# Two FNet and GLU layers on one core: the tests that stand between the matrices, spread otherwise over the steps

## The chip, the cores and the metric

One core of one Trainium2 chip runs the kernel; the other cores are idle. The metric is the device time of one execution in microseconds. Three runs of the kernel before took 1140.98, 1141.98 and 1143.59 us, so the median is 1141.98 us. One more execution was profiled and took 1143.76 us.

## The reference

Two layers, each a spectral mixing and a gated linear unit, on x of 2048 rows by 640 columns, all in float32:

```python
def _A_ref(x, dft_seq_re, dft_seq_im, dft_hid_re, dft_hid_im):
    a = jnp.einsum("bsd,ed->bse", x, dft_hid_re)
    b = jnp.einsum("bsd,ed->bse", x, dft_hid_im)
    return jnp.einsum("ts,bse->bte", dft_seq_re, a) - jnp.einsum("ts,bse->bte", dft_seq_im, b)

def _B_ref(x, w_gate, w_up, w_down):
    h = _sigmoid(jnp.einsum("bsd,df->bsf", x, w_gate)) * jnp.einsum("bsd,df->bsf", x, w_up)
    return jnp.einsum("bsf,fd->bsd", h, w_down)

for _ in range(2):
    x = x + _A_ref(_layernorm(x), ...)
    x = x + _B_ref(_layernorm(x), ...)
```

The two sequence matrices have 2048 by 2048 numbers, the two hidden matrices 640 by 640, and the three weights of the unit have 1728 hidden columns. All of them are inputs. The kernel uses that the four transform matrices are symmetric in their rows and columns, and it does not take that for granted: while it computes by the short way it tests these symmetries on the data, sums up the squares of all deviations, and at the end goes to a general way (`general`) if a flag says that one of them does not hold.

## The kernel before, in words

**The matrices.** Numbers are split into a high and a low half-precision part (HI and LO), and a product is made of three passes. The 2048 rows are four blocks (`block` holds the step at which each begins). A block has 14 steps in which gate and up values are made, two hidden chunks j to a pair of steps, and then eight steps that multiply by the third weight (`down`, matrices at L1546, drained by VectorE at L1561). Layer 1's blocks 1, 2 and 3 begin at steps 19, 41 and 63, layer 2's four blocks at steps 105, 127, 149 and 171.

**A pair of steps in TensorE's order.** For two chunks come parts one (6 matrices each) and two (9 each), then the gates of the pair before, then part four of one older chunk (9), part six twice (6 each), part four of the other (9), part five twice (6 each), part seven twice (9 each) and part three twice (9 each): 108 matrices of 128 by 256, nearly all at L1389. After parts five, six and seven ScalarE copies the sums out of PSUM (L1393, a snap). Part seven needs part six's snap, and part three needs part five's. After part three VectorE adds (L1425, L1426), which also frees the banks; ScalarE makes the gate from that (L1435). The up values go through VectorE (L1445, L1447) and are split by ScalarE (L1456) and VectorE (L1457).

**The order is written out.** The function that holds all this first lists the steps and then places small jobs with `at(u, f, ...)`: job f runs at place u, a number of steps with a fraction. When a step is emitted, its jobs are sorted by u. A down step emits them ahead of its matrices. A pair of steps has four places for them, numbered 0 to 3 by the halves of its two steps: place 0 stands behind the gates and ahead of part six, place 1 after part six, place 2 after part five, place 3 after part seven and ahead of part three. Each engine works through its own instructions in the order in which they were emitted, so a job that waits holds up what stands behind it on its engine.

**The tests.** A test has three jobs. `load_rows` or `load_cols` fetches four pieces of a sequence matrix (`in_ct`) with four DMAs that GpSimd issues (L1596, L1613). `test_rows` or `test_cols` takes differences and sums on VectorE (L1602, L1603 and L1605 twice; for columns L1619 to L1622). `square_rest` takes the oldest entry of the list `rest` and squares it on ScalarE with a running sum (L1579). The data lie in a room of 8 units of SBUF; there are two rooms, and test k uses room k modulo 2. So a load waits for the square of the test two before it. In layer 1 there are 42 tests from step 47 to step 76 and 9 more in the last phase of the layer; the load is at u, the test one pace later and the square 1.7 paces after the load, a pace being the distance between two tests. In layer 2 the rest come in three runs: 8 in block 0, 10 in block 1, 15 around block 2, the test 1.4 and the square 1.8 paces after the load.

**The hidden matrices.** `load_hidden_rows` (GpSimd) and `load_hidden_cols` (SyncE) fetch them into the same two rooms in block 2's second half and block 3; `test_hidden_rows` and `test_hidden_cols` (L1679, L1682, L1683) test them on VectorE. `test_all` makes the flag from all sums (L1693 to L1710).

**Buffers.** Everything else in SBUF that lives for a while is taken from `Slots`: a first pass over the program writes down how long each slot is held on a clock that advances with every take and give, and `find_homes` then places all slots, the largest area first.

## Time and profile before

| what | value |
|---|---|
| median of three runs | 1141.98 us |
| the profiled execution | 1143.76 us, its span 1141.9 us |
| TensorE busy | 1110.8 us, 97% |
| VectorE busy | 761.8 us, 67% |
| ScalarE busy | 537.2 us, 47% |
| GpSimd busy | 348.1 us, 30% |
| granted TensorE clock, mean | 0.996 |
| DMA | 214.72 MB, 188 GB/s in the mean |

A row of a timeline gives the start and the length of one instruction or of a run of like ones in us, the engine, the line of the kernel, the operation and its operands, and in brackets how long the engine was idle ahead of it and what ended that. A row of the costliest groups gives the busy time, the mean of one in ns, and the idle time ahead of them. A row of windows gives, after the window and its length, the busy time of TensorE, of its weight loads, of VectorE, ScalarE and GpSimd with the number of instructions, the clock, the share of the DMA engines and GB/s. Line numbers are those of the kernel before; in the changed kernel the same code stands one line further down, and beyond the test functions up to 13.

### The profile page before, as it was taken

The page shows a single profiled execution, that of the slowest core. Times are in us where ns is not written, and L with a number is a line of the kernel's source. Part 1 is how long each engine was busy: PE and PEld are TensorE (multiplying, and loading weights), DVE is VectorE, ACT ScalarE, POOL GpSimd, SP SyncE. Part 2 cuts the span into 40 slices and gives each one's busy share as a digit, 9 for nine tenths or more (in the row PEclk, how much of TensorE's full clock was granted, in tenths as well). Part 3 has the DMA queues.
Part 4 walks back from the last instruction along what each step waited for, and adds up shares of the span by engine and source line. Part 5 has one row for each costly group of instructions (what it writes and reads, how often), then busy time and mean ns, then how long its engine had stood idle before and what let it go on. Part 6 is the DMA issues. An engine that isn't in the chain of part 4 may idle for free. (4 is left out here: it accounts for less than half of the span.)

```text
span 1141.9 us, 23440 instructions
## 1 busy us (share of the span) xinstructions
PE 1110.8 (97%) x9030; PEld 882.3 (77%) x9030; DVE 761.8 (67%) x1678; ACT 537.2 (47%) x1187; POOL 348.1 (30%) x568
## 2 busy tenths in 40 slices
PE   5889999999999999999999999999999999999998
PEld 3668446788878887788878888778877888788875
DVE  7994998856756775486667878834664568526750
ACT  6975583355524653256525545315541455225430
POOL 1001664332546452432350216021453113141000
PEclk9899999999999999999999999999999999999999
DMA  8444685967495767968621665475767864499401
GB/s 250 152 124 151 240 319 157 270 210 244 154 244 182 246 185 152 246 223 291 201 98 57 177 223 160 130 216 179 241 167 174 257 230 150 85 254 284 143 18 38
DMA packets 154447, 214.72 MB, mean 188 GB/s; under 512 B 74655, under 2 KB 99505, under 8 KB 154326
## 3 DMA queue, kind: packets, MB, share of 16 engines
q1 hardware_dynamic: 135622, 165.04, 48.4%
q0 software_dynamic: 18560, 47.93, 14.3%
q8 instruction: 72, 1.18, 0.4%
q14 instruction: 49, 0.40, 0.1%
q10 hardware_dynamic: 144, 0.16, 0.0%
HBM read 173.04 MB, written 25.44 MB: 174 GB/s over the span
## 5 line engine op out<-in xcount | busy, mean ns | idle before, releaser
L1389 PE MATMUL acc<-big 128*128 128x256 f16 x4698 | 517.1, 273 | 4.7 <-ACT big L1393 4.5
L1389 PEld LDWEIGHTS <-big 128*128 128x128 f16 x4698 | 459.6, 98 | 60.1 <-issue 5.7
L1546 PE MATMUL acc<-big 128*128 128x320 f16 x2624 | 357.7, 299 | 0.0
L1546 PEld LDWEIGHTS <-big 128*128 128x128 f16 x2624 | 256.8, 98 | 99.5
L1596 POOL DMA_DIRECT2D big<-in_ct x256 | 174.5, 687 | 270.6 <-DVE big L1605 181.3
L1393 ACT ACTIVATE big<-acc 128x256 f32<-128x256 f32 x348 | 127.7, 380 | 214.7 <-PE acc L1389 212.4
L1579 ACT ACTIVATE big<-big 128x768 f32<-128x768 f32 (+10 forms) x110 | 81.6, 742 | 113.0 <-DVE big L1605 85.5
L1457 DVE TENSOR_TENSOR big<-big 128x512 f16<-128x512 f32 x87 | 59.9, 689 | 105.9 <-ACT big L1456 105.7
L1342 PE MATMUL acc<-big 128*128 128x256 f16 (+1 forms) x705 | 114.6, 325 | 0.5 <-ACT big L672 0.5
L1342 PEld LDWEIGHTS <-big 128*128 128x128 f16 x705 | 68.9, 98 | 45.0 <-issue 0.7
L1435 ACT ACTIVATE big<-big 128x512 f32<-128x512 f32 x87 | 53.3, 627 | 49.1 <-DVE big L1426 48.2
L270 DVE SCALAR_TENSOR_TENSOR big<-big 128x640 f16<-128x640 f32 (+7 forms) x82 | 62.7, 797 | 6.7 <-ACT big L268 6.6
L1561 DVE SCALAR_TENSOR_TENSOR big<-acc,big 128x320 f32<-128x320 f32 x64 | 28.4, 483 | 57.8 <-PE acc L1546 57.8
L1445 DVE SCALAR_TENSOR_TENSOR big<-acc,big 128x256 f32<-128x256 f32 x87 | 36.3, 418 | 41.7 <-PE acc L1389 36.3
L1426 DVE TENSOR_TENSOR big<-big,acc 128x512 f32<-128x512 f32 x87 | 59.2, 681 | 2.0 <-PE acc L1389 1.8
L268 ACT ACTIVATE big<-big 128x640 f16<-128x640 f32 (+7 forms) x82 | 50.9, 657 | 17.3 <-POOL big L1283 6.5
L616 ACT ACTIVATE big<-big 128x384 f16<-128x384 f32 (+2 forms) x48 | 28.8, 648 | 64.1 <-DVE big L598 45.0
L1456 ACT ACTIVATE big<-big 128x512 f16<-128x512 f32 x87 | 54.5, 626 | 9.3 <-DVE big L1447 7.3
L1613 POOL DMA_DIRECT2D big<-in_ct x40 | 27.3, 685 | 96.9 <-ACT big L1393 73.7
L1602 DVE TENSOR_TENSOR big<-big 128x256 f32<-128x256 f32 x64 | 26.7, 416 | 27.4 <-DMA big<-in_ct 26.0
L1603 DVE TENSOR_TENSOR big<-big 128x256 f32<-128x256 f32 x64 | 26.9, 420 | 21.9 <-DMA big<-in_ct 21.9
L979 PE MATMUL acc<-big 128*128 128x256 f16 (+2 forms) x288 | 34.7, 273 | 6.4 <-DVE big L270 2.5
(242 smaller groups left out, 1068.3 us busy)
## 6 DMA issues: line engine op xcount, KB each, us to landing
big<-kept_s SPq DMA_DIRECT2D x84, 512.0 KB, 5.7
big<-kept_w SPq DMA_DIRECT2D x115, 320.0 KB, 5.3
big<-in_ct POOLq DMA_DIRECT2D x256, 128.0 KB, 4.4
big<-kept_w SPq DMA_DIRECT2D x74, 192.0 KB, 6.2
kept_w<-big SPq DMA_DIRECT2D x27, 320.0 KB, 3.7
big<-in_ct POOLq DMA_DIRECT2D x32, 256.0 KB, 4.9
kept_s<-big SPq DMA_DIRECT2D x13, 512.0 KB, 5.7
big<-in_wg SPq DMA_DIRECT2D x18, 320.0 KB, 3.2
```

The costliest lines, as they stand in the source:

```text
L268: nc.scalar.activation(dh, src, AF.Copy, scale=s)
L270: nc.vector.scalar_tensor_tensor(dl, src, s, dh, op0=OP.mult, op1=OP.subtract)
L1342: nc.tensor.matmul(ps, w[wp][:, d * P : (d + 1) * P], xt[:, xp, :], start=(d == 0 and wp == HI and xp == HI), stop=(d == ND - 1 and wp == LO))
L1389: nc.tensor.matmul(ps, wt, xt, start=start and n == 0, stop=n == len(todo) - 1, skip_group_check=not start)
L1393: nc.scalar.activation(dst, ps, AF.Copy)
L1426: nc.vector.tensor_tensor(v, v, other, op=OP.add)
L1435: nc.scalar.activation(v, v, AF.Sigmoid, scale=SG)
L1456: nc.scalar.activation(s.parts[HI], v, AF.Copy)
L1457: nc.vector.tensor_tensor(s.parts[LO], v, s.parts[HI], op=OP.subtract)
L1546: nc.tensor.matmul(held["pd", e][0][:, :EH], held["ht", j].parts[hp][:, i * P : (i + 1) * P], held["w", 2, j].parts[wp][:, e * EH : (e + 1 ...
L1579: nc.scalar.activation(v, v, AF.Square, accum_out=new_sum()[:p])
L1596: nc.gpsimd.dma_start(v[:, g], bass.AP(ct.tensor, (r * S + row) * S, [[P, NS], [d * S, 16], [1, P]]))
```

## The change

Six things are edited.

- The loads no longer take room k modulo 2. `new_room` takes a free one of the two fixed rooms, and if there is none, a third of 8 units from `Slots`, under the mark LATE: such a slot does not advance the clock, and `find_homes` places it after all others. A room is given back when its square has been issued.
- In layer 1 the test comes 1.2 paces after its load instead of 1.0, the square 1.95 instead of 1.7. The paces are the same.
- In layer 2 the three runs have 4, 12 and 17 tests instead of 8, 10 and 15, over the same steps. From block 1 on the test comes 1.7 paces after the load instead of 1.4, the square 2.6 instead of 1.8.
- The tests of the hidden matrices' rows are 1.95 steps apart instead of 1.7, and each comes 3.2 steps after its load instead of 2.8. Those of their columns begin at 32 steps after block 2's start instead of 29.8, with the test 1.6 steps later instead of 1.4 and the square at 1.45 times that instead of 1.15. Three of the six column tests come to stand in the eight down steps of block 3.
- `test_all` stands two steps later.
- Where zeros and warm-up matrices used a view of the first room, they name the same place in `big`.

```diff
     def take(self, n, high):
-        self.clock += 1
-        self.asked.append([n, self.clock, None])
+        self.clock += high != LATE
+        self.asked.append([n, self.clock, None, high == LATE])
...
-    area = [n * (t1 - t0) for n, t0, t1 in asked]
+    area = [n * (t1 - t0) - 10**9 * late for n, t0, t1, late in asked]
...
+    rooms, n_room, free_rooms = {}, [], [0, 1]
     def square_rest(n=1):
         for _ in range(n):
-            square_sum(rest.pop(0))
-    def room(k, n=CK):
-        u = UNITS + CK * (k % 2)
-        return big[:, u * UNIT : (u + n) * UNIT]
+            v, done = rest.pop(0)
+            square_sum(v)
+            if done:
+                k = n_room.pop(0)
+                if k > 1:
+                    drop("room", k)
+                else:
+                    free_rooms.append(k)
+    def new_room(*key):
+        k = free_rooms.pop(0) if free_rooms else len(rooms)
+        v = take(CK, "room", k, high=LATE).f32 if k > 1 else big[:, (UNITS + CK * k) * UNIT : (UNITS + CK * (k + 1)) * UNIT]
+        rooms[key] = v
+        n_room.append(k)
+        return rooms[key]
...
-            free = (block[0] + 6, block[0] + 13, 8), (block[1] + 3, block[1] + 14, 10), (block[2] - 6, block[2] + 14, 15)
+            free = (block[0] + 6, block[0] + 13, 4), (block[1] + 3, block[1] + 14, 12), (block[2] - 6, block[2] + 14, 17)
...
+            tight = first or u0 < block[1]
             for u in [u0 + pace * k for k in range(n)]:
                 load, test, key = tests.pop(0)
                 at(u, load, *key)
-                at(u + (1.0 if first else 1.4) * pace, test, *key)
-                at(u + (1.7 if first else 1.8) * pace, square_rest)
+                at(u + (1.2 if first else 1.4 if tight else 1.7) * pace, test, *key)
+                at(u + (1.95 if first else 1.8 if tight else 2.6) * pace, square_rest)
...
-            tests = [(load_hidden_rows, test_hidden_rows, (r, k), 15.5 + 1.7 * (4 * r + k), 2.8) for r in range(2)
+            tests = [(load_hidden_rows, test_hidden_rows, (r, k), 15.5 + 1.95 * (4 * r + k), 3.2) for r in range(2)
                      for k in range(4)]
-            tests += [(load_hidden_cols, test_hidden_cols, (r, j), 29.8 + 0.9 * (3 * r + j), 1.4) for r in range(2)
+            tests += [(load_hidden_cols, test_hidden_cols, (r, j), 32 + 0.9 * (3 * r + j), 1.6) for r in range(2)
                       for j in range(3)]
...
-            at(block[3] + 16, test_all)
+            at(block[3] + 18, test_all)
```

TensorE's order has the same rows in both kernels. What moves is seen on ScalarE.

ScalarE at the start of layer 1's block 3 (steps 63 to 65): L1393 is a snap, L1579 a square, L1435 a gate. Before, with the end of the down steps ahead:

```order
L1393 ACTIVATE big<-acc_64 128x256
L1393 ACTIVATE big<-acc_438 128x256
L1579 ACTIVATE big,dsum<-big 128x768
L1393 ACTIVATE big<-acc_64 128x256
L1393 ACTIVATE big<-acc_438 128x256
L1393 ACTIVATE big<-acc_440 128x256
L1393 ACTIVATE big<-acc_439 128x256
L1393 ACTIVATE big<-acc_64 128x256
L1393 ACTIVATE big<-acc_438 128x256
L1579 ACTIVATE big,dsum<-big 128x768
L1393 ACTIVATE big<-acc_67 128x256
L1393 ACTIVATE big<-acc_437 128x256
```

The rows of the change, from the same first snap on to the gates of the next pair:

```order
L1394 ACTIVATE big<-acc_64 128x256
L1394 ACTIVATE big<-acc_438 128x256
L1580 ACTIVATE big,dsum<-big 128x768
L1394 ACTIVATE big<-acc_440 128x256
L1394 ACTIVATE big<-acc_439 128x256
L1394 ACTIVATE big<-acc_64 128x256
L1394 ACTIVATE big<-acc_438 128x256
L1394 ACTIVATE big<-acc_67 128x256
L1394 ACTIVATE big<-acc_437 128x256
L1436 ACTIVATE big<-big 128x512 x2
L1580 ACTIVATE big,dsum<-big 128x768
L1394 ACTIVATE big<-acc_67 128x256
```

The first square has moved behind two more snaps (part six's), and the second, which stood ahead of step 65's snaps of older chunks, now stands behind that pair's two gates and ahead of its part six's snaps.

ScalarE at the start of layer 2's block 2 (step 149). Before, from the first snaps to the gates of the next pair:

```order
L1393 ACTIVATE big<-acc_65 128x256
L1393 ACTIVATE big<-acc_438 128x256
L1579 ACTIVATE big,dsum<-big 128x768
L1393 ACTIVATE big<-acc_65 128x256
L1393 ACTIVATE big<-acc_438 128x256
L1393 ACTIVATE big<-acc_437 128x256
L1393 ACTIVATE big<-acc_66 128x256
L1393 ACTIVATE big<-acc_65 128x256
L1393 ACTIVATE big<-acc_438 128x256
L1579 ACTIVATE big,dsum<-big 128x768
```

The same place in the change:

```order
L1394 ACTIVATE big<-acc_65 128x256
L1394 ACTIVATE big<-acc_438 128x256
L1394 ACTIVATE big<-acc_65 128x256
L1394 ACTIVATE big<-acc_438 128x256
L1580 ACTIVATE big,dsum<-big 128x768
L1394 ACTIVATE big<-acc_437 128x256
L1394 ACTIVATE big<-acc_66 128x256
L1394 ACTIVATE big<-acc_65 128x256
L1394 ACTIVATE big<-acc_438 128x256
L1580 ACTIVATE big,dsum<-big 128x768
```

The square that stood between the first two snaps and part six's now stands behind part six's.

ScalarE at the end of layer 2's block 3 (step 183), where squares are of the hidden matrices' columns. Before:

```order
L1435 ACTIVATE big<-big 128x512 x2
L1579 ACTIVATE big,dsum<-big 128x160
L1579 ACTIVATE big,dsum<-big 128x321
L1579 ACTIVATE big,dsum<-big 1x319
L1393 ACTIVATE big<-acc_437 128x256
L1393 ACTIVATE big<-acc_67 128x256
L1456 ACTIVATE big<-big 128x512
L1579 ACTIVATE big,dsum<-big 128x160
L1579 ACTIVATE big,dsum<-big 128x321
L1393 ACTIVATE big<-acc_437 128x256
```

And in the change:

```order
L1436 ACTIVATE big<-big 128x512 x2
L1580 ACTIVATE big,dsum<-big 128x160
L1580 ACTIVATE big,dsum<-big 128x319
L1394 ACTIVATE big<-acc_437 128x256
L1394 ACTIVATE big<-acc_67 128x256
L1457 ACTIVATE big<-big 128x512
L1580 ACTIVATE big,dsum<-big 128x160
L1580 ACTIVATE big,dsum<-big 128x319
L1394 ACTIVATE big<-acc_437 128x256
```

One square fewer stands between the gates and the snaps. The squares that were here are now in the down steps behind.

More of the change, by code (lines that the diff above doesn't have):

```diff
@@ L76 @@
 NEAR = (8, 1)
+LATE = 2
 class Slots:
@@ L93, in give @@
     def give(self, s):
-        self.clock += 1
+        self.clock += not self.asked[s.k][3]
         self.asked[s.k][2] = self.clock
 def find_homes(asked):
-    area = [n * (t1 - t0) for n, t0, t1 in asked]
+    area = [n * (t1 - t0) - 10**9 * late for n, t0, t1, late in asked]
     for near in NEAR:
@@ L272, in start @@
     def start():
-        nc.gpsimd.memset(room(0, 1), 0.0)
+        nc.gpsimd.memset(big[:, UNITS * UNIT : (UNITS + 1) * UNIT], 0.0)
         nc.gpsimd.memset(dsum, 0.0)
@@ L371, in junk @@
     def junk(n):
-        v = room(0, 1).bitcast(F16)
+        v = big[:, UNITS * UNIT : (UNITS + 1) * UNIT].bitcast(F16)
         for _ in range(n):
@@ L1598, in test_rows @@
     def test_rows(r, k):
-        v = room(k)
+        v = rooms[r, k]
         a, b, c, d = (v[:, 2 * P * g : 2 * P * (g + 1)] for g in range(4))
@@ L1605, in test_rows @@
             nc.vector.tensor_tensor(c[:, odd::2], a[:, odd::2], c[:, odd::2], op=other if odd else same)
-        rest.append(v[:, 2 * P :])
+        rest.append((v[:, 2 * P :], True))
     def load_cols(r, i, k):
         n, row = (P, START[i]) if i < NB else (1, SB)
-        v = room(k).rearrange("p (g c) -> p g c", g=4)[:n]
+        v = new_room(r, i, k).rearrange("p (g c) -> p g c", g=4)[:n]
         for g, t in ((0, 1 + 256 * k), (2, HS - 256 * (k + 1))):
@@ L1615, in test_cols @@
     def test_cols(r, i, k):
-        v = room(k)[: P if i < NB else 1]
+        v = rooms[r, i, k][: P if i < NB else 1]
         a, d, c, b = (v[:, 256 * g : 256 * (g + 1)] for g in range(4))
@@ L1622, in test_cols @@
         nc.vector.tensor_tensor(c, c, a[:, ::-1], op=other if i in (2, 3) else same)
-        rest.append(v[:, 256:])
+        rest.append((v[:, 256:], True))
     def load_edges(r):
@@ L1652, in load_hidden_rows @@
     def load_hidden_rows(r, k):
-        v = room(k)[: 20 * ND].rearrange("p (g n c) -> p g n c", g=2, c=P)
+        v = new_room("rows", r, k)[: 20 * ND].rearrange("p (g n c) -> p g n c", g=2, c=P)
         for g, (row, d) in enumerate(((1 + 80 * k, 1), (D - 1 - 80 * k, -1))):
@@ L1658, in test_hidden_rows @@
     def test_hidden_rows(r, k):
-        a, b = (room(k)[: 20 * ND, 4 * P * g : 4 * P * (g + 1)] for g in range(2))
+        a, b = (rooms["rows", r, k][: 20 * ND, 4 * P * g : 4 * P * (g + 1)] for g in range(2))
         nc.vector.tensor_tensor(b, a, b, op=OP.subtract if r == 0 else OP.add)
-        rest.append(b)
+        rest.append((b, True))
     def turns():
@@ L1969, in folded @@
                 at(block[2] + u + later, test, *key)
-                at(block[2] + u + 1.15 * later, square_rest, 1 if load is load_hidden_rows else 3 if key == (1, 0) else 2)
-            at(block[3] + 16, test_all)
+                at(block[2] + u + (1.15 if load is load_hidden_rows else 1.45) * later, square_rest, 1 if load is load_hidden_rows else 3 if key == (1, 0) else 2)
+            at(block[3] + 18, test_all)
     for u, step in enumerate(steps):
```

16 lines of the change are left out of this document (8 added, 8 removed).

## The prediction

> **What bounds the kernel now.** The page's first parts come first, then the groups.
> ```profile
> span 1141.9 us, 23440 instructions
> PE 1110.8 (97%) x9030; PEld 882.3 (77%) x9030; DVE 761.8 (67%) x1678; ACT 537.2 (47%) x1187; POOL 348.1 (30%) x568
> ...
> PEclk9899999999999999999999999999999999999999
> ...
> L1389 PE MATMUL acc<-big 128*128 128x256 f16 x4698 | 517.1, 273 | 4.7 <-ACT big L1393 4.5
> ...
> L1546 PE MATMUL acc<-big 128*128 128x320 f16 x2624 | 357.7, 299 | 0.0
> L1393 ACT ACTIVATE big<-acc 128x256 f32<-128x256 f32 x348 | 127.7, 380 | 214.7 <-PE acc L1389 212.4
> ```
> TensorE is busy 97% of the span, at full clock from the third slice on. The matrices of the down phase (L1546) never wait. Those of the transforms (L1389) are late by 4.7 us in all, 4.5 of it behind ScalarE's copies out of PSUM, which I call snaps (L1393). Only such gaps can be won or lost, since the change leaves every TensorE instruction where it was. The list of TensorE's waits and its timeline, around each gap, show where they are.
> ```profile
> PE twin L399 <- DMA big<-in_x: 12.6, 4, 6.5
> PE acc L1389 <- ACT big L1393: 4.5, 6, 1.4
> ```
> ```profile
> 476.32 2.78 PE L1389 MATMUL acc<-big 128*128 128x256 f16 x24 [0.89 <-ACT big L1393]
> 480.52 16.64 PE L1389 MATMUL acc<-big 128*128 128x256 f16 x151 [1.42 <-ACT big L1393]
> 709.16 2.45 PE L1389 MATMUL acc<-big 128*128 128x256 f16 x21 [0.42 <-ACT big L1393]
> 891.94 8.24 PE L1389 MATMUL acc<-big 128*128 128x256 f16 x74 [1.17 <-ACT big L1393]
> 1033.12 49.32 PE L1389 MATMUL acc<-big 128*128 128x256 f16 x450 [0.18 <-DVE big L1426]
> 1088.43 2.13 PE L1389 MATMUL acc<-big 128*128 128x256 f16 x18 [0.42 <-ACT big L1393]
> 1090.76 1.14 PE L1389 MATMUL acc<-big 128*128 128x256 f16 x9 [0.20 <-ACT big L1393]
> ```
> Columns: start, duration, then in brackets the idle time ahead and what ended it. Six gaps end with a snap: 0.89, 1.42, 0.42, 1.17, 0.42 and 0.20, in sum 4.52. The seventh, 0.18, ends with a VectorE add of the transform itself. The opening's 12.6 us wait for x and are not touched. So all that can be won is 4.52 us. For each gap I read what ScalarE did just before.
>
> **Term 1, 476.32, stays.** ScalarE's timeline at layer 1's block 3, and VectorE's and a window beside it:
> ```profile
> 475.07 0.84 ACT L1579 ACTIVATE big<-big 128x768 f32<-128x768 f32 x1 [3.83 <-DVE big L1605]
> 475.82 0.19 ACT L1579 ACTIVATION_READ_ACCUMULATOR big<-big 128x1 f32 x1
> 479.26 0.84 ACT L1579 ACTIVATE big<-big 128x768 f32<-128x768 f32 x1 [2.72 <-DVE big L1605]
> 480.11 1.19 ACT L1393 ACTIVATE big<-acc 128x256 f32<-128x256 f32 x4
> 484.84 0.84 ACT L1579 ACTIVATE big<-big 128x768 f32<-128x768 f32 x1 [1.77 <-DVE big L1605]
> 489.44 0.63 ACT L1435 ACTIVATE big<-big 128x512 f32<-128x512 f32 x1 [3.09 <-DVE big L1426]
> 490.37 0.63 ACT L1435 ACTIVATE big<-big 128x512 f32<-128x512 f32 x1 [0.30 <-DVE big L1426]
> 490.90 0.64 ACT L1393 ACTIVATE big<-acc 128x256 f32<-128x256 f32 x2
> ```
> ```profile
> 478.23 0.42 DVE L1603 TENSOR_TENSOR big<-big 128x256 f32<-128x256 f32 x1 [1.46 <-DMA big<-in_ct]
> 488.67 0.68 DVE L1426 TENSOR_TENSOR big<-big,acc 128x512 f32<-128x512 f32 x1
> 489.60 0.68 DVE L1426 TENSOR_TENSOR big<-big,acc 128x512 f32<-128x512 f32 x1
> ...
> 479.00:492.00 13.00, 11.58 (x107) 10.28 (x106) 12.73 (x34) 6.26 (x17) 5.93 (x12) 1.00 0.57 172
> ```
> A square (L1579, 0.84 plus 0.19) waits on its test, and the snaps of the new block's first matrices stand behind it in ScalarE's order. That is the gap of 0.89. In the change this square, its test and the load stand in the same order: 0.00.
>
> **Term 2, 480.52, goes and comes back: −0.1.** The same again: the test of the next columns waits for its load until 478.23, its square ends at 480.11, four snaps are late, TensorE stands 1.42 us. In the change this square is behind two of those snaps (the rows ahead of this prediction), so the gap goes. But the square that ran at 484.84 in an idle stretch moves too, behind the two gates (L1435). The gates wait for VectorE's adds, which end at 489.35 and 490.28 and are not bound by TensorE: VectorE is busy 12.73 of the 13.00 us from 479 to 492 (the window's row, third busy time), with the same work ahead of the adds in both kernels. So the gates still end at about 490.9, the moved square takes 0.95 (0.84 and 0.19 overlapping), and the two snaps behind it start at 491.85 instead of 490.90. The seventh part's first matrix needs the first of them, 0.38 long: 492.25. Before, TensorE came there 108 matrices after 480.52, each 0.1095 (49.32 us for 450, less the last one's tail): 492.34. Bounds: −1.42 if the adds come early, +0.5 if the square is late itself. I take −0.1, since these rows fix it.
>
> **Terms 3 and 4, 709.16 and 891.94, go: −0.42 and −1.17.** ScalarE's rows before the two gaps, and VectorE's and GpSimd's before the second:
> ```profile
> 707.91 0.84 ACT L1579 ACTIVATE big<-big 128x768 f32<-128x768 f32 x1 [3.81 <-DVE big L1605]
> 708.75 0.36 ACT L1393 ACTIVATE big<-acc 128x256 f32<-128x256 f32 x1
> ...
> 890.68 0.84 ACT L1579 ACTIVATE big<-big 128x768 f32<-128x768 f32 x1 [4.07 <-DVE big L1605]
> 891.52 1.19 ACT L1393 ACTIVATE big<-acc 128x256 f32<-128x256 f32 x4
> ```
> ```profile
> 889.64 0.43 DVE L1603 TENSOR_TENSOR big<-big 128x256 f32<-128x256 f32 x1 [1.11 <-DMA big<-in_ct]
> ...
> 879.70 3.42 POOL L1596 DMA_DIRECT2D big<-in_ct  x5
> ```
> At 709 the last square of layer 2's block 0 is ahead of one snap. The change puts four tests there instead of eight, so none is at this place: −0.42, upper bound 0. At 891.94 a square waits on a test whose four loads were issued from 879.70 on and landed at 889.6, 7 us after the last issue. In the change the squares of this step stand behind the sixth part's snaps, and each comes longer after its test (2.6 paces instead of 1.8). A load landing 2 us later would still do: −1.17, upper bound 0.
>
> The Trainium skill, "DMA: Bandwidth & Descriptors", section "Anatomy of one DMA — SWDGE (gpsimd) path", gives 2.0 us plus the bytes at 436 GB/s, about 2.3 us for 128 KB. By it the last of the four loads is there at 884.7 (879.70 + 4 × 0.68 + 2.3), the test waits no longer than that, and term 4 has nothing to win: the sum would be −1.14, 1140.8. The row of 889.64 speaks against it here, so the sum stays.
>
> **Term 5, 1088.43 and 1090.76, go: −0.62.** ScalarE at the end of layer 2's block 3, and VectorE:
> ```profile
> 1086.80 0.32 ACT L1579 ACTIVATE big<-big 128x160 f32<-128x160 f32 x1
> ...
> 1087.58 0.45 ACT L1579 ACTIVATE big<-big 1x319 f32<-1x319 f32 x1
> ...
> 1088.03 0.62 ACT L1393 ACTIVATE big<-acc 128x256 f32<-128x256 f32 x2
> ```
> ```profile
> 1103.75 0.28 DVE L1693 TENSOR_REDUCE fin<-dsum 128x1 f32<-128x128 f32 x1
> ```
> Three squares of the hidden matrix take 1.23 us ahead of the snaps, the third 0.45 of it. In the change two stand there, so the snaps start 0.45 earlier against a gap of 0.42, and fewer tests have gone through VectorE by then. The second gap follows a pair of squares too; its test is earlier in the change. Bounds 0 and −0.62. The tests that move into the down phase meet no L1546 that waits (0.0 above). The last reckoning starts at 1103.75; two down steps later is some 9 us (44.72 us of the last stretch hold eight steps' matrices), long before the span's end: 0.
>
> **The third room: 0.** It takes 11 loads out of the two fixed rooms' turn. Other buffers change places only from layer 2's block 3 on. Were a slab's load held up by a square, the price would be one landing, 5.7 us; the first use there is several steps away.
> ```profile
> big<-kept_s SPq DMA_DIRECT2D x84, 512.0 KB, 5.7
> ```
>
> **Sum:** −0.1 − 0.42 − 1.17 − 0.62 = −2.31. The profiled execution took 1143.76 us (span 1141.9 and 1.86 around it), so 1141.45. It lies 1.78 over the median of the runs, 1141.98, so the forecast is **1139.7 us**. A measurement of this kernel tells about 0.2% from no change, 2.28 us: the forecast lies on that bound.
>
> **Rivals.** *A, the second gap is not given back* (VectorE's adds come early enough, or snaps pass): −1.32 more, 1138.4. For it: the adds follow TensorE in other steps. Against: the idle-free VectorE rows.
> *B, it does less than it says*: loads land later in the change's places too, and squares again stand before snaps; only term 3 and the first gap of term 5 remain, −0.84, 1141.1. For it: a landing of 7 us where the page has 4.4 for the median is not excluded elsewhere.
> *C, slower: squares between the gates and the snaps behind them.* There are 14 such places in the change, 19 before, but six are new (layer 1's steps 31, 43, 49 and 65, layer 2's 155 and 159). A place costs nothing while the gates end within 7.9 − 0.95 − 0.38 = 6.5 us of the step's start; from there up to 0.95. The heaviest stretch is this:
> ```profile
> 940.00:960.00 20.00, 20.00 (x186) 17.92 (x184) 18.73 (x46) 9.35 (x22) 6.63 (x18) 1.00 0.47 162
> 800.00:820.00 20.00, 20.00 (x186) 17.92 (x184) 12.67 (x33) 11.62 (x27) 8.71 (x13) 1.00 0.90 277
> ```
> VectorE is busy 18.73 of 20 us (third busy time), and TensorE all of it. With the other five places over the point: +4.75 − 2.31 = +2.4, 1144.4. Against: step 159's gates end at about 5.9 us by these rows.
> *D, transfers.* Layer 2's block 1 gets two more tests, 1.05 MB, where the DMA share is 0.90 at 277 GB/s (second row): if TensorE's weights wait for them, +3.8, so 1143.5. Against: no L1389 waits for a DMA anywhere. The Trainium skill, same page, section "Queues, rings and completion order", says that each engine takes packets from its queues in turn, so the loads would take the weights' share at once; that gives this rival's 3.8 whole, and no run here shows it.
>
> **How the numbers follow.** Forecast 0.52, A 0.18, B 0.15, C 0.10, D 0.05. The forecast's own range is 1138.6 to 1140.9; slightly more than half of it (0.30) I count as faster, as small gains at steps without a visible gap are likelier than losses. Faster 0.30 + 0.18 = 0.48; slower C's 0.10; within 0.2% the rest, 0.42. The range goes from below A, 1137.8, to between B and D, 1142.8.
>
> **What would show it.** TensorE's timeline of the changed kernel should have the gap at 476 and none at 480; a small one near 492 at step 65, after a gate and a square; none at the end of layer 2's block 0, at the start of block 2 and at the end of block 3. TensorE's waits on L1393's successor should sum to 2.2 to 2.4 (0.89 plus about 1.4). If 492 has no gap, A is right; if squares show as idle TensorE time elsewhere, C; if "DMA" ends a wait of the transforms, D. The prediction is wrong altogether if the sum of TensorE's waits is as before and the time is not.

## The result, and the profile after

The changed kernel took 1139.03 us in the median of 18 runs (1138.25 to 1141.29), the kernel before 1141.13 us in 18 runs made beside it (1140.08 to 1145.24). The ratio is 0.9979, 95% interval 0.9972 to 0.9987: 2.1 us by the medians, 2.4 by the ratio. The forecast was 1139.7 us and −2.31. It is about the 0.2% that was called the bound of what can be told, with the whole interval below 1.

The page of the changed kernel, its first lines and the groups that answer to those of before:

```profile
span 1139.5 us, 23456 instructions
PE 1110.4 (97%) x9030; PEld 883.1 (78%) x9030; DVE 761.8 (67%) x1678; ACT 538.5 (47%) x1187; POOL 348.8 (31%) x568
...
L1390 PE MATMUL acc<-big 128*128 128x256 f16 x4698 | 516.6, 273 | 1.8 <-ACT big L1394 1.4
...
L1547 PE MATMUL acc<-big 128*128 128x320 f16 x2624 | 357.7, 299 | 0.0
```

The busy times are the same within 1.3 us. What has changed is the idle time ahead of the transforms' matrices, 1.8 us instead of 4.7. TensorE's waits and its timeline at the places of the prediction:

```profile
PE acc L1390 <- ACT big L1394: 1.4, 1, 1.4
...
PE acc L1390 <- DMA big<-kept_w: 0.4, 1, 0.4
```

```profile
472.85 17.85 PE L1390 MATMUL acc<-big 128*128 128x256 f16 x162
492.06 8.13 PE L1390 MATMUL acc<-big 128*128 128x256 f16 x73 [1.36 <-ACT big L1394]
...
708.32 2.46 PE L1390 MATMUL acc<-big 128*128 128x256 f16 x21
...
883.87 16.32 PE L1390 MATMUL acc<-big 128*128 128x256 f16 x148
...
1031.19 49.30 PE L1390 MATMUL acc<-big 128*128 128x256 f16 x450 [0.42 <-DMA big<-kept_w]
...
1085.89 3.11 PE L1390 MATMUL acc<-big 128*128 128x256 f16 x27
```

Rows without a bracket are work that follows without a gap. The gaps at 709, 892, 1088 and 1090 are gone. So is the one at 480, and 1.36 us came at 492, as forecast. Two things were not forecast: the gap at 476 is gone as well, and at 1031 TensorE now waits 0.42 us for a weight's load. So TensorE's waits behind snaps sum to 1.4, not to the 2.2 to 2.4 that was named as the sign. This profiled execution took 1141.29 us, 2.26 over the median of the 18.

Since the opening differs from execution to execution, I set the traces side by side by the start of the same matrix, counted from the first matrix of L1342 behind the opening (84.92 us before, 85.77 after):

| matrix (its place in the profile before) | before | after | what the stretch from the row above lost or won |
|---|---|---|---|
| 476, block 3 of layer 1 | 391.40 | 390.35 | −1.05 |
| 480, part seven | 395.60 | 392.97 | −1.58 |
| 492, part seven of step 65 | 407.39 | 406.28 | +1.52 |
| 709, end of layer 2's block 0 | 624.24 | 622.54 | −0.59 |
| 892, start of block 2 | 807.01 | 803.99 | −1.32 |
| 1033, step 173 | 948.19 | 945.42 | +0.25 |
| 1088, end of block 3 | 1003.51 | 1000.12 | −0.62 |
| 1090 | 1005.84 | 1002.09 | −0.36 |
| last matrix | 1051.24 | 1047.49 | 0.00 |

From the matrix at 492 on, the changed kernel is 2.64 us shorter. A gap in the timeline is a little smaller than the step it makes here (0.42 shown, 0.59 stepped), since the profile models the ends of matrices.

One correction to the section on the kernel: layer 1's 42 tests run from step 25 to step 76, 1.21 steps apart, not from step 47.

### The profile page after: what moved, and what is told of

It reads as the page before. It is cut to its first block, busy times and chain, and to the rows that moved or that the text cites. A ratio compares the mean times of both kernels' runs of the same rounds, so it can differ in the third digit from the quotient of the medians.

```text
span 1139.5 us, 23456 instructions
## 1 busy us (share of the span) xinstructions
PE 1110.4 (97%) x9030; PEld 883.1 (78%) x9030; DVE 761.8 (67%) x1678; ACT 538.5 (47%) x1187; POOL 348.8 (31%) x568
## 5 line engine op out<-in xcount | busy, mean ns | idle before, releaser
L1394 ACT ACTIVATE big<-acc 128x256 f32<-128x256 f32 x348 | 130.3, 382 | 233.2 <-PE acc L1390 229.6
L438 POOL DMA_INDIRECT out<-big,rows x8 | 9.5, 1182 | 125.5 <-DVE fin L1705 55.1
```

What stands on the lines that cost most here:

```text
L1394: nc.scalar.activation(dst, ps, AF.Copy)
```

## The experiments

Each was timed beside the kernel before on the same chip. The groups e1 to e4, e5 to e7, f and g ran on four different chips, so across groups only the ratios to the kernel before are compared. The line of the program that each edits is the changed kernel's. The table tests are those of the sequence matrices, and the last reckoning is `test_all`.

**Layer 1's factors alone (e1).**

```diff
-free = (block[0] + 6, block[0] + 13, 4), (block[1] + 3, block[1] + 14, 12), (block[2] - 6, block[2] + 14, 17)
+free = (block[0] + 6, block[0] + 13, 8), (block[1] + 3, block[1] + 14, 10), (block[2] - 6, block[2] + 14, 15)
-at(u + (1.2 if first else 1.4 if tight else 1.7) * pace, test, *key)
+at(u + (1.2 if first else 1.4) * pace, test, *key)
```

(likewise the square at 1.95 and 1.8, and the hidden matrices and `test_all` as before)

> Only layer 1's two factors of the change (test 1.2, square 1.95 paces after the load); layer 2 as before. My theory, the sum of the gaps: the gap of 1.42 us at 480 goes and one of about 1.4 us comes at step 65 (492), so the change of time is -0.1 us, between -0.3 and +0.1. Of the gap at 476, theory A (the place is timed by the tests' loads, and a late opening is taken up there): gap and opening add up, so the matrix behind it starts at 476.1 to 476.4 whatever the opening lost, as in both profiles (476.32 and 476.12), and the time from the opening's end to it shrinks by just what the opening lost. Rival B (the new factors bring the loads forward): that matrix starts earlier than 476.0 when the opening is as quick as in the kernel before, and the whole is about 0.9 us faster.

Measured: 1140.54 us, ratio 0.9998 (0.9989 to 1.0007). No change clear of noise, as the sum of the gaps had it. VectorE's row of the last piece of test (0,30), and TensorE's row at step 65:

```profile
477.05 0.43 DVE L1615 TENSOR_TENSOR big<-big 128x256 f32<-128x256 f32 x1 [0.72 <-DMA big<-in_ct]
...
491.13 53.87 PE L1390 MATMUL acc<-big 128*128 128x256 f16 x492 [0.81 <-ACT big L1394]
```

The matrix at 476 started 390.36 behind the opening (475.75 − 85.39). Theory A fails: this matrix was not at 476.1 to 476.4. Rival B is not settled by this run. Its first half holds here, since the matrix came ahead of 476.0 with an opening that ended 0.47 us later than before, and the interval does not exclude its 0.9 us. But in e3 below, with layer 1 as before, the same matrix also stands 390.35 behind the opening, so the new factors are not what brings it forward.

**Layer 2's table tests alone (e2).** Layer 1 at 1.0 and 1.7, the hidden matrices and `test_all` as before.

```diff
-15.5 + 1.95 * (4 * r + k), 3.2
+15.5 + 1.7 * (4 * r + k), 2.8
-32 + 0.9 * (3 * r + j), 1.6
+29.8 + 0.9 * (3 * r + j), 1.4
```

> Only layer 2's table tests of the change (4, 12 and 17 tests, 1.7 and 2.6 paces from block 1 on, the third room); layer 1 and the hidden matrices as before. My theory: the gaps at 709 (0.42) and at 891.94 (1.17) go, the two at 1088 and 1090 (0.62) stay: -1.6 us, with the steps of the traces a little larger (-0.59 and -1.33 in the two profiles) -1.9 us. Rival: the gaps at the end of block 3 go with these tests too, because the fixed rooms come free otherwise: -2.2 to -2.9 us. The new wait of 0.42 us for a weight's load at 1031 shows here if it comes from the third room's place in memory, and not if it comes from the hidden matrices' loads.

Measured: 1146.41 us, ratio 1.0049 (1.0036 to 1.0062): 5.6 us slower than before, where I had expected 1.6 to 1.9 faster. TensorE's timeline, then ScalarE's and VectorE's rows at the new gap, then the windows around it:

```profile
1015.11 15.09 PE L1390 MATMUL acc<-big 128*128 128x256 f16 x112 [3.57 <-ACT big L1394]
...
1089.48 2.13 PE L1390 MATMUL acc<-big 128*128 128x256 f16 x18 [0.42 <-ACT big L1394]
```

```profile
1014.07 0.63 ACT L1580 ACTIVATE big<-big 100x512 f32<-100x512 f32 x1 [6.69 <-DVE big L1672]
1014.60 0.19 ACT L1580 ACTIVATION_READ_ACCUMULATOR big<-big 100x1 f32 x1
1014.70 1.18 ACT L1394 ACTIVATE big<-acc 128x256 f32<-128x256 f32 x4
...
1013.34 0.69 DVE L1672 TENSOR_TENSOR big<-big 100x512 f32<-100x512 f32 x1 [13.11 <-DMA big<-in_wh]
```

```profile
1015.00:1021.00 6.00, 5.89 (x30) 4.14 (x30) 0.00 (x0) 1.65 (x6) 1.63 (x2) 0.53 0.97 201
1021.00:1027.00 6.00, 6.00 (x58) 5.37 (x56) 3.29 (x7) 2.57 (x7) 2.31 (x2) 1.00 0.89 295
```

The gaps at 709 and 892 are gone here (the stretches from 492 to 709 and on to 892 are 0.58 and 1.33 us shorter than before), those at 1088 and 1090 stay: that half of the theory holds. But at the start of block 3 the square of a hidden row test stands ahead of snaps and waits for its test, the test for its load. TensorE stands 3.57 us, and then the granted clock is 0.53 for 6 us: 30 matrices where the next window has 58. The kernel before has the same order there, and its TensorE came later to it (1016.4 instead of 1011.5), when the square was done; its test had also begun earlier (1011.57 instead of 1013.34).

**The hidden matrices and the last reckoning alone (e3).** All table tests as before (the first diff, with 1.0 and 1.7 in layer 1); the hidden matrices as changed.

> Only the hidden matrices' tests and the last reckoning of the change; all table tests as before. My theory: the gaps at 1088 and 1090 go (0.62 us shown, 0.97 in the steps of the traces), those at 480, 709 and 891.94 stay: -0.6 to -1.0 us. Rival: these gaps came from the squares of table tests late in block 3, so they stay and the time is the same. The new wait of 0.42 us at 1031 shows here if it comes from the hidden matrices' loads; then the gain is 0.2 to 0.4 us less.

Measured: 1140.19 us, ratio 0.9986 (0.9977 to 0.9995), −1.6 us. TensorE's timeline:

```profile
472.22 28.00 PE L1390 MATMUL acc<-big 128*128 128x256 f16 x255
...
706.75 2.45 PE L1390 MATMUL acc<-big 128*128 128x256 f16 x21 [0.41 <-ACT big L1394]
...
889.95 65.66 PE L1390 MATMUL acc<-big 128*128 128x256 f16 x600 [1.60 <-ACT big L1394]
...
1085.47 3.11 PE L1390 MATMUL acc<-big 128*128 128x256 f16 x27
```

The gaps at the end of block 3 are gone, those of the table tests stay. These gaps come back in each profile of a kernel that has the old tests of that part: 0.33 to 0.42 us at 709 and 1.17 to 1.60 at 892 (before, e1, e3), 0.42 and 0.20 at 1088 and 1090 (before, e1, e2). So they belong to the kernel and not to one execution. The measured gain is more than the theory's −0.6 to −1.0, but the interval takes that in. The first row was the surprise: layer 1 is that of the kernel before, and from 472 to 500 there is no gap at all.

**One square moved back (e4).**

```diff
-at(u + (1.95 if first else 1.8 if tight else 2.6) * pace, square_rest)
+at(u + (1.94 if first else 1.8 if tight else 2.6) * pace, square_rest)
```

> The whole change with layer 1's square 1.94 instead of 1.95 paces after its load: four squares change places, among them the one that stood between step 65's gates and the snaps behind them, which goes back to the idle stretch ahead of part three. My theory, that this square alone gives back what was won at 480: the gap of 1.36 us at 492 goes down to 0.4 or less, and the time is 1.0 to 1.4 us less than the changed kernel's, 3.1 to 3.8 less than before. Rival: VectorE's adds bound that place, so a gap of 1 us or more stays at 492 with the square gone, and the time is that of the changed kernel.

Measured: 1139.18 us, ratio 0.9984 (0.9975 to 0.9994), no gain over the change. In this profile the gap at 492 is gone, and one has come at 476, where nothing was edited:

```profile
474.23 0.43 DVE L1615 TENSOR_TENSOR big<-big 128x256 f32<-128x256 f32 x1 [2.06 <-DMA big<-in_ct]
...
476.52 68.28 PE L1390 MATMUL acc<-big 128*128 128x256 f16 x624 [1.47 <-ACT big L1394]
```

Its runs lie from 1137.12 to 1142.59, those of the change from 1138.25 to 1141.29. Both ways fell in part: the gap at 492 went as the theory said, and the time stayed as the rival said. What the gaps hang on had to be something that differs by execution.

**The change without layer 1's part (e5).** Factors 1.0 and 1.7 in layer 1, all else as changed.

> The whole change except layer 1's two factors, which are those of the kernel before (1.0 and 1.7). The first runs gave a new theory: the gaps at 476 and 480 are there only in executions in which the tests' loads land late (the kernels with layer 1 as before had none in their profiles), while the gap at 492 is made by the change in each. By it this kernel has no gap at 492, and its profile has at 476 and 480 together anything from 0 to 2.3 us; its median is 0.3 to 1.3 us less than the changed kernel's (0.9968 to 0.9977 of before), its runs lie wider apart. Rival, the prediction's own account: the gap of 1.42 at 480 is there in every run, so the median is within 0.3 us of the changed kernel's.

Measured: 1140.74 us, ratio 0.9990 (0.9981 to 0.9998). I expected it to be quicker than the change, and it was not; the intervals of the two overlap. Its profile:

```profile
476.47 0.43 DVE L1615 TENSOR_TENSOR big<-big 128x256 f32<-128x256 f32 x1 [0.49 <-DMA big<-in_ct]
...
478.76 65.66 PE L1390 MATMUL acc<-big 128*128 128x256 f16 x600 [0.85 <-ACT big L1394]
...
1030.53 49.30 PE L1390 MATMUL acc<-big 128*128 128x256 f16 x450 [1.16 <-DMA big<-kept_w]
```

This kernel is e2 with the hidden matrices' tests and the last reckoning as changed. It has 0.9990 where e2 has 1.0049, and the gap at 1015 is gone, so these tests are what made e2 slow. It is also e3 with layer 2's table tests as changed, and there its time shows nothing of the 1.6 us of terms 3 and 4: 0.9990 where e3 has 0.9986. The two traces show where they went. From the matrix at 492 to the one at 892 e5 takes 2.32 us less than e3, and from there to the one at 1033 it takes 1.42 us more, with the wait of 1.16 us in the last row.

With this the layer-1 places can be ordered by one number, the start of the last piece of test (0,30) on VectorE, which waits for its load. Both columns are counted from the opening's end (for e5 476.47 − 84.78):

| kernel | layer 1 | test (0,30), last piece | matrix at 492 | difference |
|---|---|---|---|---|
| before | before | 393.31 | 407.39 | 14.08 |
| after | changed | 392.20 | 406.28 | 14.08 |
| e5 | before | 391.69 | 405.77 | 14.08 |
| e1 | changed | 391.66 | 405.74 | 14.08 |
| e2 | before | 390.84 | 404.92 | 14.08 |
| e3 | before | 389.89 | 404.76 | no gap |
| f3 (below) | changed | 388.76 | 404.76 | no gap |
| g2 (below) | changed | 388.52 | 404.76 | no gap |

In these eight profiles the landing of that load sets the time, whichever of the two orders stands in the program; the order only decides where the gap is seen, at 480 or at 492. With no late load the matrix comes at 404.76. The gap at 476 hangs in the same way on the test ahead, (0,29). Its last piece starts at 389.11 in the kernel before and at 389.69 in e4, the only two with a gap there, and the matrix follows 2.3 us later; in the other seven it starts at 388.04 or earlier, and the matrix comes at 390.35 or 390.36. The kernel e4 is not in the table, because it has a third order: its test (0,30) starts at 392.64 and its matrix at 492 comes 13.75 us later, held up by the gap at 476 and not by a square of step 65. How late the load is differs from execution to execution of kernels that are alike up to there.

**Longer times in layer 1 too (e6).**

```diff
-at(u + (1.2 if first else 1.4 if tight else 1.7) * pace, test, *key)
-at(u + (1.95 if first else 1.8 if tight else 2.6) * pace, square_rest)
+at(u + (1.7 if first else 1.4 if tight else 1.7) * pace, test, *key)
+at(u + (2.6 if first else 1.8 if tight else 2.6) * pace, square_rest)
```

> The whole change, and layer 1's tests also get the longer times that use the third room: the test 1.7 paces after the load, the square 2.6. If the gaps at 476 and 480 come from loads that land late, the loads now have 12 us instead of 7 to 9 before their test, and no gap is left at 476, 480 or 492 (the moved square of step 65 stands behind part six there): 1.0 to 2.0 us less than the changed kernel, a ratio to before of 0.996 to 0.997, and runs that lie closer together. Rival: these gaps come from VectorE's chain of work at the start of block 3 whatever the loads do; then a gap of 1 us or more stays near 480 or 492 and the time is that of the changed kernel. A third way: the third room in layer 1 moves other buffers, and weights come late somewhere else: a DMA ends a wait of the transforms.

Measured: 1140.78 us, ratio 0.9993 (0.9984 to 1.0002). All gaps from 476 to 492 are gone, in this profile and in those of f1, f2 and g1, which have the same layer 1. But a DMA now ends two waits of TensorE, and the clock fell behind the second:

```profile
554.34 0.83 PE L980 MATMUL acc<-big 128*128 128x255 f16 x6 [0.84 <-DMA big<-kept_o]
...
1031.15 50.71 PE L1390 MATMUL acc<-big 128*128 128x256 f16 x450 [2.67 <-DMA big<-kept_w]
...
1030.00:1040.00 10.00, 8.85 (x69) 7.39 (x69) 3.55 (x7) 3.20 (x9) 1.90 (x2) 0.83 1.04 322
```

The wait at 1031 is the third way of the expectation. The one at 554 is there in f1, f2 and g1 too (0.42 to 0.58 us), and in these four the stretch from 492 to 709 takes 0.65 to 1.09 us more than in the change. So e6 came to the matrix at 892 only 0.44 us earlier than the change. It waited 2.67 us at 1031 and not 0.42 mainly because the weight landed later, 947.17 us after the opening's end instead of 945.37. Why it did is not shown. This profiled execution was also the slowest of its twelve (1142.07, the median 1140.78), so not all of these waits need be the kernel's.

**The hidden rows' spacing without that of the columns (e7).** As e2, with the rows at 1.95 and 3.2.

> Layer 2's table tests as changed, and of the hidden matrices only the row tests (1.95 steps apart, 3.2 after the load); their columns, the last reckoning and layer 1 as before. Theory: the gap of 3.57 us at 1015, which made the table tests alone slower, comes from one square of a hidden row test that stands at step 171 ahead of the snaps and waits for its load; with the rows' new spacing it stands behind them, so this gap and the slower matrices behind it are gone: 5 to 7 us less than the table tests alone, 1.5 to 2.5 less than before (ratio 0.998), with the gaps at 1088 and 1090 still there. Rival: the gap at 1015 comes from the table tests' late squares or the third room, so it stays and the kernel is slower than before.

Measured: 4221.3 us. The kernel went the general way behind its own end, so its time says nothing of the theory. Here the first column's test comes ahead of the last rows', so rooms are given back in another order than they were taken; that this spoiled the data under test is argued, not shown. The stretch up to there can be read:

```profile
1018.37 11.96 PE L1390 MATMUL acc<-big 128*128 128x256 f16 x108 [1.05 <-DMA big<-kept_w]
...
1087.75 2.12 PE L1390 MATMUL acc<-big 128*128 128x256 f16 x18 [0.43 <-ACT big L1394]
...
1153.31 46.88 PE L2060 MATMUL acc<-big 128*128 128x512 f32 x104 [17.53 <-DMA big<-in_ct]
```

The gap of 3.57 us behind a square is not there, with the same table tests as in e2 and only the rows respaced; a wait of 1.05 us for a weight has come, two new gaps behind snaps stand at 1076 and 1081 (0.67 and 0.82), and the gap at the end of block 3 is as before. So far as one stretch of one trace goes, of the hidden matrices' tests it is the rows' spacing that takes the gap of e2 away.

**Without the hidden rows' tests (f1).** As e6, with `for r in range(0)` in the rows' list: their eight loads, tests and squares are left out.

> The kernel with the longer times and the third room in layer 1 (e6), with the eight tests of the hidden matrices' rows left out: no loads, no tests, no squares of them. Theory: the waits for a weight's load at 1031 (0.42 us in the changed kernel, 1.16 and 2.67 us where it reaches this place earlier) come from the transfers around it, which are at their limit from 1000 to 1040 us, and the hidden rows' loads are part of them; so without them the wait is under 0.3 us, the matrices behind it are not slowed, and the kernel takes 1137 to 1138.5 us, 2.5 to 3.5 less than e6. Rival: the wait comes from the order in which SyncE issues the loads of weights behind a buffer that comes free late; then it stays at 1 us or more without the hidden rows.

Measured: 1138.17 us, ratio 0.9973 (0.9962 to 0.9984), 2.3 us less than e6. TensorE runs through the place, and the DMA engines have room there. The row of TensorE and two windows of f1, then the same two windows of the change:

```profile
1014.83 30.40 PE L1390 MATMUL acc<-big 128*128 128x256 f16 x277
...
1010.00:1020.00 10.00, 10.00 (x94) 8.96 (x93) 2.10 (x4) 4.11 (x10) 0.00 (x0) 1.00 0.29 95
1020.00:1030.00 10.00, 10.00 (x94) 8.97 (x92) 4.10 (x10) 3.84 (x9) 0.00 (x0) 1.00 0.62 220
```

```profile
1010.00:1020.00 10.00, 10.00 (x94) 8.96 (x92) 2.65 (x5) 3.74 (x12) 5.20 (x5) 1.00 1.05 267
1020.00:1030.00 10.00, 10.00 (x94) 8.95 (x93) 3.54 (x8) 5.04 (x13) 2.31 (x2) 1.00 1.03 301
```

The last but one number of a window is the DMA share, 0.29 and 0.62 instead of 1.05 and 1.03. Between 1000 and 1035 us a weight's load of 320 KB lands 3.3 us after its issue in f1 and 9.3 in the change, in the median. So the wait at 1031 comes from the hidden rows' loads. The rival falls as it was worded, since the wait did not stay; SyncE's part in it is small but not nothing, for the weight of this place was issued at 1017.8 in f1 and at 1019.5 in e6.

**The hidden rows elsewhere (f2, f3, g1, g2).** Four tests a step apart at the end of block 2 and four late in block 3, on e6 (f2) and on the change (f3); then all eight late in block 3, on e6 (g1) and on the change (g2). In all four the columns' tests and the last reckoning come two steps later (not in the cuts below).

```diff
-15.5 + 1.95 * (4 * r + k), 3.2
+15.5 + 14.5 * r + k, 2.0
```

> e6 with the hidden matrices' rows elsewhere: four of the eight tests one step apart from 15.5 steps after block 2's start on, and the other four from 30 on, out of the stretch from 1000 to 1050 us; columns two steps later, the last reckoning too. By the same theory as for the kernel without these tests, the wait at 1031 is under 0.5 us: 2 to 3.5 us less than e6, 0.5 to 1.5 less than the changed kernel, 1137.5 to 1138.5. Rival (order of the weights' loads): 1 us or more is waited at 1031. A risk is the end of block 3, where four row tests now lie: gaps like those at 1088 of the kernel before would cost up to 1 us.

> The whole change with layer 1 as the change has it (1.2 and 1.95) and the hidden matrices' tests spread as in f2. If the gains ahead of 1000 us are capped by the wait at 1031, this kernel, which reaches it later than f2 by the gap at 492 (0.8 to 1.4 us), has no wait there and is 0.2 to 0.5 us faster than the changed kernel (0.42 us of wait gone), and slower than f2 by about 1 us. Rival: no difference to the changed kernel (within 0.1%).

Measured: 1157.38 us (1.0144, 1.0124 to 1.0165) and 1157.73 us (1.0138, 1.0121 to 1.0156). In f3 TensorE waits for the transposes at the start of block 3, 5.03 us in the first of the rows ("issue" means that the profile shows nothing it waited for) and 11.13 in the second. TensorE's rows and SyncE's of f3, then SyncE's of the change:

```profile
1011.96 0.37 PE L1390 MATMUL acc<-big 128*128 128x256 f16 x1 [5.03 <-issue]
1023.46 73.32 PE L1390 MATMUL acc<-big 128*128 128x256 f16 x653 [11.13 <-DMA big<-big]
...
996.29 15.56 SPq L624 DMA_TRANSPOSE big<-big  x2
```

```profile
997.78 7.19 SPq L624 DMA_TRANSPOSE big<-big  x2
```

SyncE's row of the last transposes is twice as long, and the last of them landed 21.4 us after its issue, in the change 5.6. Four hidden loads were issued from 993.5 to 997.0 in f3, two (995.0 and 996.2) in the change. The expectations missed this place; they say nothing of the wait at 1031, which came long after.

```diff
-15.5 + 1.95 * (4 * r + k), 3.2
+30 + 0.5 * (4 * r + k), 1.2
```

> e6 (layer 1's tests 1.7 and squares 2.6 paces after the load) with all eight row tests of the hidden matrices late in block 3, from 30 steps after block 2's start, half a step apart, the test 1.2 steps after the load; columns from 34 on, the last reckoning two steps later. The kernel without the row tests had no wait at 1031 and took 1138.17 us; by the theory of the transfers this one has none there either, and takes 1138.0 to 1139.0, 0.1 to 0.3% less than before by the same measure as it (0.9973 to 0.9983). Rival: the row tests on VectorE and ScalarE between 1060 and 1090 bring back the gaps at 1088 and 1090 (0.6 to 1.0 us) or the loads hold up the weights of steps 177 to 183; then 1139 to 1140.5.

> The same place of the row tests, with layer 1 as the change has it. Against the kernel above it differs in layer 1 alone. Theory: with layer 1's shorter times some executions have 0.8 to 1.6 us of gaps between 476 and 492 and some none, and nothing later takes this up any more, so the median is 0.3 to 1.2 us over the kernel above, with a wider spread. Rival: layer 1's times make no difference (within 0.2 us), or the wait of 0.4 to 0.8 us at 554, which all kernels with the third room in layer 1 showed, outweighs them, and this one is the faster.

Measured: 1143.28 us (1.0023, 1.0010 to 1.0035) and 1143.66 us (1.0014, 1.0005 to 1.0023), and neither is quicker than the other by more than the intervals. The wait at 1031 is gone in both, but squares of the moved tests now stand ahead of snaps and wait. TensorE, ScalarE and VectorE of g1 (in g2 the longest of these gaps is 3.10 us):

```profile
1073.25 3.76 PE L1390 MATMUL acc<-big 128*128 128x256 f16 x33 [0.65 <-ACT big L1394]
1079.13 1.97 PE L1390 MATMUL acc<-big 128*128 128x256 f16 x9 [2.11 <-ACT big L1394]
...
1078.08 0.63 ACT L1580 ACTIVATE big<-big 100x512 f32<-100x512 f32 x1 [4.09 <-DVE big L1672]
...
1077.36 0.69 DVE L1672 TENSOR_TENSOR big<-big 100x512 f32<-100x512 f32 x1 [1.97 <-DMA big<-in_wh]
```

No version that does the whole work beat the change.

## Why the prediction was right, point by point

- **Terms 3, 4 and 5 (−0.42, −1.17, −0.62)** were right in their mechanism, and each gap hangs on its own part: e2 removes the first two and keeps the third, e3 the other way round. In the steps of the traces they are −0.59, −1.32 and −0.98, so the three were sized 0.68 us too small. As a time of their own the gains of terms 3 and 4 are not shown: between e3 and e5 the time shows nothing of them, and in their traces 1.42 of 2.32 us are lost again by 1033.
- **Terms 1 and 2 (0 and −0.1)** were right in the sum, and e1 measured 0.9998 for them. The chain of term 2 was right too: from the last piece of test (0,30) to the matrix at 492 it has 14.02 us (478.23 to 492.25), and 14.08 were measured. That the matrix came at 492.06, so near to 492.25, is luck, for the opening ended 0.85 us later and the load came 1.11 us earlier behind it. And the premise was wrong that the gaps at 476 and 480 belong to the kernel before. They belong to the execution that was profiled: with the same layer 1, e3 has neither and e5 only 0.85 us at 480. The sizes agree with that: the profiled execution was 2.63 us over the median of 18, and its matrix at 492 was late by 407.39 − 404.76 = 2.63 us. To the last digit this is chance, since the opening's end alone lies anywhere from 83.93 to 85.77 us in these traces. Had I counted these gaps as won and also taken off the difference to the median, I would have counted them twice.
- **Rival A** (the gap at 480 is not given back) fell in the change's profile, which has the gap at 492. It holds only for executions whose load lands early, and those gain nothing at 480 either.
- **Rivals B and C** fell: the squares of terms 3 to 5 no longer hold up snaps, and in the change's profile no square between gates and snaps cost anything at the new places other than step 65.
- **The third room and the hidden rows, 0 in the sum**, were mis-sized, both ways. The prediction gave the spacing of the rows no term; yet with the old hidden tests the table tests cost 5.6 us instead of winning (e2). And the rows' loads cost 0.25 us at 1033 in the change. In e5, where TensorE gets there 0.5 us sooner, the wait is 1.16 us; in e6, where the weight also landed 1.8 us later, 2.67. That is rival D's mechanism, loads of tests ahead of weights, at another place and by other loads than it named: block 3 and the hidden rows, not block 1. The prediction said that no matrix waits for a DMA. That was true of the kernel before, whose matrix came at 948.19; the weights that were waited for landed at 945.37 (the change), 945.70 (e5) and 947.17 (e6).
- **Adding up terms as if they were independent** was right by luck: e1, e2 and e3 make −0.2, +5.6 and −1.6 us, which is not the −2.4 of the whole. Part of the luck is that the 0.68 us too little for terms 3 to 5 and the 0.25 us left out at 1033 have opposite signs.
- **Two figures of the working** are off without touching the sum: by the 44.72 us for eight down steps two of them take 11.2 us, not 9, and 7.9 − 0.95 − 0.38 is 6.57, not 6.5.

What stays open: why the load of test (0,30) lands up to 3.7 us apart in executions of kernels that are alike up to there. Part of it is the issue of the last of its four pieces, from 383.85 (f3) to 387.96 (before) after the opening's end, and part the time from issue to landing, from 3.88 us (e3) to 6.16 (the change). Open is also whether the 1.3 us by the ratios between e5 and the change, whose intervals overlap, are real; e1 gives layer 1's factors 0.2.

## What to carry to other kernels

A gap in one profiled execution can be a fact of that execution alone. Before you count it as the kernel's, look whether it comes back in other profiles of the same code, and whether the profiled run lies over the median by about its size. An instruction that waits and stands ahead of what the busy engine needs is the thing to look for, and moving it by one place in its queue can win or lose microseconds; price every such place again when what is ahead of it gets quicker. Gains in front of a stretch in which the DMA engines are full are kept only as far as the data lands earlier too: e5 won 2.32 us ahead of such a stretch and lost 1.42 of them in it.

## What the runs showed of the hardware

- **The clock falls after some short idle times.** Around the gap of 3.57 us in e2 the granted clock was 0.53 over 6 us; behind one of 2.11 us in g1 nine matrices took 1.97 us (1.14 in the row of 1090.76 of the kernel before), and behind one of 2.67 in e6 the clock was 0.83 over 10 us. Behind gaps of 1.60 us (e3) and less in the transforms nothing is seen: 600 matrices took 65.66 us, as they did elsewhere. But the length of the gap alone does not decide: in g2 nine matrices took 1.14 us behind a gap of 3.10. In each of the 14 traces the granted clock changes only on a grid of 3.41 us, at 1.00 or 0.50. Laying TensorE's idle time on that grid gives a rule for these traces. Where TensorE stood 2.02 us or more within one such stretch at full clock, the next stretch was at half clock, in all 43 cases; where it stood 1.81 or less, in none; and in between it went both ways (1.87 fell in e5, 1.87 and 1.99 did not in g2). The gap of g1 lies within one stretch, that of g2 is split over two. Two windows of g1, then two of g2 (busy time of TensorE after the length, the clock in the last place but two):

```profile
1075.86:1079.27 3.41, 1.30 (x13) 1.01 (x12) 0.69 (x1) 1.19 (x5) 0.93 (x1) 1.00 0.85 113
1079.27:1082.68 3.41, 3.41 (x18) 2.35 (x17) 2.78 (x6) 2.05 (x6) 1.64 (x4) 0.50 0.61 125
...
1075.47:1078.88 3.41, 1.54 (x15) 1.23 (x13) 0.54 (x1) 0.00 (x0) 0.00 (x0) 1.00 0.92 142
1078.88:1082.30 3.42, 2.19 (x21) 1.96 (x21) 1.57 (x4) 1.88 (x6) 2.56 (x4) 1.00 0.37 90
```

The Trainium skill, "TensorE: Matmul & The Clock Gate", section "What's actually happening", has half rate after an idle window of about 3.4 us. The grid agrees with that length, but e2, e6 and g1 fell after 2.30, 2.18 and 2.11 us of idle time in one stretch.
- **Transposes by DMA and loads beside them can slow each other.** SyncE's row of the first pair ahead of block 3 is 5.93 us in f1, without hidden loads, and 13.51 in the change, where two hidden loads were issued beside it; these landed after 12.6 and 13.1 us, and after 5.7 and 5.5 in the kernel before, where they had landed ahead of the pair. It is not so each time: the second pair has 7.05 us in f1 and 7.19 in the change, again with two loads beside it.
- **A load's landing is not a constant.** The same four pieces of test (0,30) were there from 388.52 to 393.31 us after the opening's end, and this alone set the time of a stretch to 0.01 us in five kernels.
